# Attention scores by eight array tiles and the state's read by four column groups, from the third batch on

## The chip, the cores and the metric

The kernel runs on one core of one Trainium2 chip. The metric is the device time of one execution in microseconds (us); three runs of the kernel before gave a median of 699.95 us (699.75 to 700.57). A core has five engines that run beside each other and wait for each other by semaphores: TensorE (PE in the profile; its weight loads are PEld), VectorE (DVE), ScalarE (ACT), GpSimd (POOL) and SyncE (SP), which issues the DMA transfers.

## The reference

There are 8 batches of 8 heads, with 512 tokens of 64 numbers each, and a state of 32 rows per head. Attention goes both ways, and its result goes through two products with `h - tanh(h)` between them.

```python
scores = scale * np.matmul(x, state.transpose(0, 1, 3, 2))      # 512 x 32 per head
a = softmax(scores)                                             # over the state's rows
xread = np.matmul(a, state)
scores2 = scale * np.matmul(state, x.transpose(0, 1, 3, 2))     # 32 x 512 per head
a2 = softmax(scores2)                                           # over the tokens
sread = np.matmul(a2, x)                                        # 32 x 64 per head
x = concatenate([xread, sread], axis=2)                         # 4608 rows of 512 after a reshape
h = x @ w_in                                                    # 512 -> 2048
g = h - np.tanh(h)
out = g @ w_out                                                 # 2048 -> 512
```

## The kernel before, in words

The main loop goes over nine chunks of output rows: one for each batch's 512 tokens, and one for the 256 rows of all state reads. A chunk has 16 steps `f`, one for each 128 columns of the hidden layer. In each step `hidden` makes a tile `hps` of h (lines 355 to 357, six matmuls of 512 columns in three passes over float32r parts), ScalarE and VectorE make `g` of it (`finish`, lines 363, 89, 90), and `output` adds its share to the four tiles `ops` (lines 393 to 395, twelve matmuls of 512 columns). Between these stand the products of `m_units` (`mps`, lines 185 and 186), which make state @ w_in for later batches, and the attention of the next batch.

Attention of batch b works on half the heads at a time (`hf` is 0 or 1; tile names carry both digits, so `sps70` is batch 7, half 0). It has three kinds of TensorE work, all in plain float32, where one product is two records of the trace, one for each of its two passes:

- the scores `sps` (line 249): per half two products, each with the 64 columns of two heads as weights and 512 tokens as moving data. The weights `bdr` hold two heads' states in blocks, so that 128 rows carry two heads of 64 numbers, with zeros beside each block. The two products of a half stand in the two halves of the array's columns.
- the transposes `pps` (line 301), four per half,
- the state's read `rps` (line 309): per half four steps over 128 tokens, and in each two products of 64 weight columns and 128 moving columns, one in each half of the array's columns. Of the 64 x 128 block that results, two diagonal 32 x 64 blocks are used (line 315).

The scores go to PSUM tiles of the pool `ps_a`, which has two banks; ScalarE copies them out (line 255), and both softmaxes start from the copies. The tables of steps in the kernel say in which step each piece of attention is made. Within that, a scheduler that is part of the framework sets the order of the instructions on each engine when the program is built, by its own model of their times.

Of the kernel before, what the change touches and what calls it, by code (L numbers as in the profile page):

```python
# [9 lines left out]
F32 = mybir.dt.float32  # L10
# [9 lines left out]
P = 128  # L20
# [6 lines left out]
EPS = 1e-9  # L27
LAG = 2


@with_exitstack
def attention_ffn(ctx: ExitStack, tc: tile.TileContext, xT, xn, bd, sp, sm, sl, win, wout, xout, sout):
    """Two-way softmax attention between x and a small state, then h - tanh(h) between two products.

    Float32 operands of the products are split exactly into two float32r parts (hi + lo, 12 bits
    each); hi*hi + hi*lo + lo*hi carry float32's accuracy in three passes.

    x's read of the state is a @ state, so its product with w_in is taken as a @ (state @ w_in),
    whose contraction is half as long.

    win and wout are float32, or float64 as int64 words, which are rounded to float32 here.
    """
    nc = tc.nc
# [24 lines left out]
    sr = [cpool.tile([P, DM], F32, name=f"sr{g}") for g in range(2)]  # L68
    # state @ w_in, [half of the heads, head, row, column]; of the last two batches, two addends
    mdram = [  # L70
# [16 lines left out]
    def split(hi, lo, src, sub=None):  # L87
        """src = hi + lo."""
        nc.scalar.copy(hi, src)  # L89
        return (sub or nc.vector).tensor_sub(lo, src, hi)  # L90

    class Weight:
        """A [P, 512] part of a weight: load() issues its load, convert() makes float32 of it."""

# [15 lines left out]
        def steps(self, dst):  # L110
            """convert() by engines: Vector's first and second part, Scalar's, GpSimd's."""
            if self.src.dtype == F32:
                return [lambda: None] * 3 + [lambda: nc.gpsimd.tensor_copy(dst, self.raw)]
            low, high = self.raw[:, :, 0], self.raw[:, :, 1]
            u, i = dst.bitcast(U32), dst.bitcast(I32)
            r = pool.tile([P, 512], I32, tag="cr", name=f"{self.name}r", bufs=CB)
            return [
                # sign, the exponent's top bit; its other seven bits, 20 bits of the fraction
                lambda: nc.vector.tensor_scalar(u, high, 3, 0x3FFFFFFF, ALU.logical_shift_left, ALU.bitwise_and),  # L119
                lambda: nc.vector.scalar_tensor_tensor(u, high, 0xC0000000, u, ALU.bitwise_and, ALU.bitwise_or),  # L120
                # the fraction's last three bits, rounded; the sum may carry into the exponent
                lambda: nc.scalar.activation(r, low, AF.Copy, scale=2.0**-29),
                lambda: nc.gpsimd.tensor_add(i, i, r),
            ]

        def convert(self, dst):
            for step in self.steps(dst):
                step()

# [1 line left out]
    m_first = {}  # L131
# [9 lines left out]
    def m_first_two(q, p):  # L141
        """Heads 2p and 2p + 1 of the first two batches, in float32 as it stands."""
        k, c = p // 2, p % 2
        if p == 0:
            # The first batch's part stays on chip.
            m_first[q] = pool.tile([P, 2, 512], F32, tag="mr", name=f"mr0{q}", bufs=RRB)
        ps = bank(ps_a, f"mps0{q}{p}")
        nc.tensor.matmul(ps, sps[:, p], wfs[q, k][:, c], start=True, stop=True)
        nc.scalar.copy(m_first[q][64 * c : 64 * c + 64, k], ps[0:64])
        stage = pool.tile([P, 2, 512], F32, tag="stage", name=f"st0{q}{p}", bufs=SB)  # L150
        nc.scalar.copy(stage[64:128, 0], ps[64:128])
        nc.sync.dma_start(
            mdram[1][q][0][k, 2 * c : 2 * c + 2].rearrange("h n f -> (h n) f"), stage[64:128, 0]
        )

    def m_units(g):
        """Of the next four batches (g = 0) and of the last two (g = 1), by pairs of heads.

        The columns of the last two batches' product: half of them by the state's hi, half by its lo.
        """  # L160
        raw = pool.tile([P, H, P], F32, tag="stage", name=f"smr{g}", bufs=SB)
# [7 lines left out]
        for q in range(NQ):  # L169
            for k in range(2):  # L170
                w = pool.tile([P, 2, 512], F32, tag="wf", name=f"w1{g}{q}{k}", bufs=WB)
                nc.sync.dma_start(w, wf[q][:, 2 * k : 2 * k + 2])
                for c in range(2):
                    p = 2 * k + c
                    # Even heads: hi over lo; odd heads: lo over hi.
                    t = twins(f"wst{g}{q}{p}", [P, 2, 512], F32R)
                    split(t[0:64, 0], t[64:128, 0], w[0:64, c], WSUB)
                    split(t[64:128, 1], t[0:64, 1], w[64:128, c], WSUB)
                    hs = slice(2 * c, 2 * c + 2)
                    stage = pool.tile([P, 2, 512], F32, tag="stage", name=f"st{g}{q}{p}", bufs=SB)  # L180
                    for e in range(2):
                        h = 2 * p + e
                        ps = bank(ps_a, f"mps{g}{q}{h}")
                        if g == 0:
                            nc.tensor.matmul(ps, s[:, 1, h], t[:, e], start=True, stop=False)  # L185
                        nc.tensor.matmul(ps, s[:, 0, h], t[:, e], start=(g == 1), stop=True)  # L186
                        nc.scalar.copy(stage[:, e], ps)  # L187
                    for j in range(4):
                        dst = mdram[2 + j][q][0] if g == 0 else mdram[6 + j % 2][q][j // 2]
                        nc.sync.dma_start(dst[k, hs].rearrange("h n f -> n h f"), stage[32 * j : 32 * j + 32])  # L190
                    yield
# [38 lines left out]

# [1 line left out]
    def attention(b, aT):  # L232
        """Products in float32 as it stands, two at a time in halves of the array's columns."""
        bdr = pool.tile([P, 4, 64], F32, tag="bdr", name=f"bdr{b}", bufs=1)
        with tc.issue_after(loadlog[min(len(loadlog) - 1, XH1)]):
            nc.sync.dma_start(bdr, bd[b])
        xrs, ss, es = [], [], []
# [8 lines left out]
        def scores(hf):  # L246
            pss[hf] = bank(ps_a, f"sps{b}{hf}")
            for c in range(2):
                nc.tensor.matmul(pss[hf][64 * c : 64 * c + 64], bdr[:, 2 * hf + c], xrs[hf][:, c], start=True, stop=True)  # L249

        for hf in range(2):
            scores(hf)
            ps = pss[hf]
            s = pool.tile([P, 512], F32, tag="s", name=f"s{b}{hf}")
            nc.scalar.copy(s, ps)
            ss.append(s)
            # over the state's rows, for x's read: 32x32 blocks transposed
            e = pool.tile([P, 16, 32], F32, tag="e", name=f"e{b}{hf}")
# [21 lines left out]
    def state_read(b, ss):  # L280
# [3 lines left out]
        for hf in range(2):  # L284
            # over the tokens, for the state's read
            s = ss[hf]
# [17 lines left out]
            yield  # L304
            ps = bank(ps_a, f"rps{b}{hf}")[:, :P]
            for k in range(4):
                for c in range(2):
                    cs = slice(64 * c, 64 * c + 64)
                    nc.tensor.matmul(  # L309
                        ps[cs], pt[:, k, cs], xr[:, k, P * c : P * c + P], start=(k == 0), stop=(k == 3)  # L310
                    )
            for j in range(4):
# [3 lines left out]
                    sr[b // 4][32 * (b % 4) : 32 * (b % 4) + 32, 64 * h : 64 * h + 64],  # L316
                    ps[js, 64 * (j % 2) : 64 * (j % 2) + 64],
                    ri[js],
# [12 lines left out]

# [1 line left out]
    class Chunk:  # L333
# [9 lines left out]
        def hidden(self, f):  # L343
            """h, then g = h - tanh(h), of 128 columns of w_in; tokens along the free axis."""
            i, n = self.i, self.n
# [22 lines left out]
        def output(self, f):  # L368
# [3 lines left out]
            if self.i == B and f >= NFF - 2:  # L372
                # The end: the first tile is stored while the second is computed.
                if f == NFF - 1:
# [50 lines left out]

    # start: what the first chunk needs
    w0 = [
        [Weight(win[r * P : r * P + P, 512 * q : 512 * q + 512], f"w{q}{r}") for r in range(DM // P)]
        for q in range(NQ)
    ]  # L430
    # The first quarter by blocks of 128 columns.
    w0[0] = [
# [11 lines left out]

    # Loads in the order of their use: w_in's quarters ahead of w_out's rows.
    loads = iter(
# [7 lines left out]

    # The start, in this order on each engine.
    firstDVE = [None]
# [33 lines left out]
    def step(op):  # L490
# [70 lines left out]
        elif k == "R":  # L561
            # the second batch's part
            if j % 2 == 0:
# [141 lines left out]
```

## Time and profile before

| what | value |
|---|---|
| time, median of 3 runs | 699.95 us (699.75 to 700.57) |
| the profiled execution, first to last instruction | 699.7 us |
| PE busy | 670.6 us, 96% of the span |
| PEld busy | 530.2 us, 76% |
| DVE busy | 464.8 us, 66% |
| ACT busy | 378.4 us, 54% |
| POOL busy | 79.2 us, 11% |
| data moved by DMA | 99.68 MB, 142 GB/s on average |
| mean granted TensorE clock | 0.982 |

The busy times are of one profiled execution, whose own time is its span; the median of the runs is 0.25 us more. Engines overlap, so busy times don't add up to the span. A matmul's end is modelled in the trace and lies behind the start of the next one, so the pace of TensorE is read from starts, not from durations.

### The profile page before, as it was taken

How to read it: one execution, taken by the hardware profiler on the slowest of the kernel's cores; microseconds unless marked ns; L12 is line 12 of the kernel's file. 1: busy time of each engine (PE TensorE's matmuls, PEld its weight loads, DVE VectorE, ACT ScalarE, POOL GpSimd, SP SyncE). 2: the span in 40 equal slices, each digit the busy share in tenths (PEclk: the TensorE clock that was granted, in tenths of full speed). 3: DMA queues.
4: the chain of work that ended last, by engine and by line, in shares of the span. 5: the costliest groups of instructions: out<-in, count | busy, mean ns of one | idle time of the engine just before them, and what ended most of it. 6: DMA issues, size and time to landing. Idle time of an engine off the chain costs nothing.

```text
span 699.7 us, 8842 instructions
## 1 busy us (share of the span) xinstructions
PE 670.6 (96%) x3146; PEld 530.2 (76%) x3146; DVE 464.8 (66%) x755; ACT 378.4 (54%) x663; POOL 79.2 (11%) x59
## 2 busy tenths in 40 slices
PE   5888995999999999999999999999999999999997
PEld 2555663888778887888788878887888788888896
DVE  5998899965695559556776558545864596444442
ACT  3876866566674655447656545543543354333442
POOL 3766656200000000000000000000000000000000
PEclk9989899899999999999999999999999999999999
DMA  8887762553554554245635632563241312001400
GB/s 298 291 298 273 250 248 100 186 199 111 152 168 141 164 163 128 90 151 151 186 120 163 170 99 65 177 189 111 77 173 61 112 69 91 30 1 38 143 31 31
DMA packets 46316, 99.68 MB, mean 142 GB/s; under 512 B 6208, under 2 KB 12096, under 8 KB 46272
## 3 DMA queue, kind: packets, MB, share of 16 engines
q1 hardware_dynamic: 46272, 99.11, 43.9%
q8 instruction: 25, 0.41, 0.3%
q14 instruction: 19, 0.16, 0.1%
HBM read 67.11 MB, written 31.98 MB: 142 GB/s over the span
## 4 chain that ended last, share of the span: by engine, by line
PE 84%; DVE 9%; ACT 2%; issue 2%; POOL 1%; DMA 1%; SPq 0%; ACTq 0%; DVEq 0%; POOLq 0%
PE ops L395 17%; PE ops L393 17%; PE ops L394 16%; PE hps L356 9%; PE hps L355 9%; PE hps L357 8%; PE rps L309 2%; PE mps L186 2%; DVE w L120 2%; PE sps L249 2%; PE mps L185 1%; DMA w01d<-in_win 1%; PE pps L301 1%; DVE wor L119 1%; DVE w L119 1%
## 5 line engine op out<-in xcount | busy, mean ns | idle before, releaser
L393 PE MATMUL ops<-wo,g 128*128 128x512 f32 x544 | 211.1, 398 | 4.8 <-ACT wo L89 2.9
L394 PE MATMUL ops<-wo,g 128*128 128x512 f32 x544 | 215.1, 395 | 0.2 <-POOL wo L90 0.2
L395 PE MATMUL ops<-wo,g 128*128 128x512 f32 x544 | 208.9, 394 | 0.0
L363 ACT ACTIVATE t<-hps 128x512 f32<-128x512 f32 (+1 forms) x142 | 81.3, 573 | 151.3 <-PE hps L357 150.7
L363 DVE TENSOR_TENSOR t<-hps,t 128x512 f32<-128x512 f32 (+1 forms) x142 | 93.2, 658 | 102.3 <-ACT t L363 101.3
L393 PEld LDWEIGHTS ops<-wo,g 128*128 128x128 f32 x544 | 103.0, 190 | 32.7 <-ACT wo L89 4.6
L90 DVE TENSOR_TENSOR g<-t,g 128x512 fp32r<-128x512 f32 (+1 forms) x142 | 100.2, 706 | 39.9 <-ACT g L89 37.9
L89 ACT CAST g<-t 128x512 fp32r<-128x512 f32 (+1 forms) x142 | 84.7, 596 | 72.7 <-DVE t L363 69.8
L394 PEld LDWEIGHTS ops<-wo,g 128*128 128x128 f32 x544 | 103.0, 189 | 23.3 <-issue 2.3
L395 PEld LDWEIGHTS ops<-wo,g 128*128 128x128 f32 x544 | 103.4, 190 | 22.5 <-issue 0.5
L355 PE MATMUL hps<-aT,m 128*128 128x512 f32 x248 | 99.5, 402 | 3.3 <-DVE t L363 1.7
L357 PE MATMUL hps<-aT,m 128*128 128x512 f32 x248 | 98.4, 399 | 0.7 <-DVE m L90 0.7
L356 PE MATMUL hps<-aT,m 128*128 128x512 f32 x248 | 98.5, 398 | 0.0
L355 PEld LDWEIGHTS hps<-aT,m 128*128 128x128 f32 x248 | 47.3, 191 | 15.3 <-ACT m L89 2.4
L90 DVE TENSOR_TENSOR wst<-w,wst 64x512 fp32r<-64x512 f32 x64 | 46.0, 718 | 19.2 <-ACT wst L89 15.9
L356 PEld LDWEIGHTS hps<-aT,m 128*128 128x128 f32 x248 | 47.5, 191 | 11.7 <-issue 2.2
L357 PEld LDWEIGHTS hps<-aT,m 128*128 128x128 f32 x248 | 47.4, 191 | 11.7 <-DVE m L90 1.5
L90 DVE TENSOR_TENSOR m<-mr,m 128x1024 fp32r<-128x1024 f32 x31 | 39.9, 1287 | 9.4 <-ACT m L89 9.3
L187 ACT COPY st<-mps 128x512 f32<-128x512 f32 x64 | 36.7, 587 | 14.6 <-PE mps L186 14.3
L89 ACT CAST wst<-w 64x512 fp32r<-64x512 f32 x64 | 39.6, 619 | 2.3 <-issue 1.5
L89 ACT CAST m<-mr 128x1024 fp32r<-128x1024 f32 x31 | 32.3, 1042 | 3.6 <-DMA mr<-md 3.4
L90 POOL TENSOR_TENSOR wo<-wor,wo 128x512 fp32r<-128x512 f32 x16 | 25.3, 1586 | 6.0 <-ACT wo L89 6.0
(216 smaller groups left out, 661.7 us busy)
## 6 DMA issues: line engine op xcount, KB each, us to landing
md<-st SPq DMA_DIRECT2D x144, 128.0 KB, 2.3
mr<-md SPq DMA_DIRECT2D x28, 512.0 KB, 4.0
xT<-in_xT SPq DMA_DIRECT2D x16, 512.0 KB, 4.4
xn<-in_xn SPq DMA_DIRECT2D x16, 512.0 KB, 4.8
w<-wf SPq DMA_DIRECT2D x16, 512.0 KB, 4.9
out_x<-ob SPq DMA_DIRECT2D x32, 256.0 KB, 2.2
wn<-wf SPq DMA_DIRECT2D x8, 512.0 KB, 3.9
ml<-md SPq DMA_DIRECT2D x8, 512.0 KB, 3.6
```

The source lines that it names most:

```text
L89: nc.scalar.copy(hi, src)
L90: return (sub or nc.vector).tensor_sub(lo, src, hi)
L119: lambda: nc.vector.tensor_scalar(u, high, 3, 0x3FFFFFFF, ALU.logical_shift_left, ALU.bitwise_and),
L120: lambda: nc.vector.scalar_tensor_tensor(u, high, 0xC0000000, u, ALU.bitwise_and, ALU.bitwise_or),
L187: nc.scalar.copy(stage[:, e], ps)
L355: nc.tensor.matmul(ps, mhi[k][:, cols], ahi[:, k], start=(k == 0), stop=False)
L356: nc.tensor.matmul(ps, mhi[k][:, cols], alo[:, k], start=False, stop=False)
L357: nc.tensor.matmul(ps, mlo[k][:, cols], ahi[:, k], start=False, stop=(k == nk - 1))
L363: tanhs.append((nc.scalar.activation(t, ps, AF.Tanh).ins, nc.vector.tensor_sub(t, ps, t).ins))
L393: nc.tensor.matmul(o, g[:, 0, tok], wo[:, f, 0], start=(f == 0), stop=False)
L394: nc.tensor.matmul(o, g[:, 0, tok], wo[:, f, 1], start=False, stop=False)
L395: return nc.tensor.matmul(o, g[:, 1, tok], wo[:, f, 0], start=False, stop=(f == NFF - 1)).ins
```

## The change

Batches 0 and 1 stay as they are (`LONE = 2`). From batch 2 on:

- Scores: each product takes one head alone, with its 64 numbers as rows and its 32 state rows as weight columns. The first four heads stand in the upper 64 rows of the array and the last four in the lower 64, each in a column group of its own, so that eight products stand in eight tiles of 64 rows and 32 columns. All eight are issued by one function, and both `sps` banks are taken at once. The weights have no zeros any more, and their load is half as large (64 KB instead of 128 KB). The inputs are laid out for that on the host.
- State's read: each step of 128 tokens has four products of 32 weight columns and 64 moving columns, one in each column group, instead of two of 64 and 128. The useful blocks are the same, and no others are computed.

```diff
-        bdr = pool.tile([P, 4, 64], F32, tag="bdr", name=f"bdr{b}", bufs=1)
+        if b < LONE:
+            bdr = pool.tile([P, 4, 64], F32, tag="bdr", name=f"bdr{b}", bufs=1)
+        else:
+            bdr = pool.tile([P, 4, NS], F32, tag="bdr", name=f"bdr{b}", bufs=1)
         with tc.issue_after(loadlog[min(len(loadlog) - 1, XH1)]):
-            nc.sync.dma_start(bdr, bd[b])
+            nc.sync.dma_start(bdr, bd[b] if b < LONE else bh[b - LONE])
...
+        def all_scores():
+
+            pss.update({hf: bank(ps_a, f"sps{b}{hf}") for hf in range(2)})
+            for j in range(4):
+                for hf in range(2):
+                    rs = slice(64 * hf, 64 * hf + 64)
+                    nc.tensor.matmul(
+                        pss[hf][32 * j : 32 * j + 32], bdr[rs, j], xrs[j // 2][rs, j % 2], start=True, stop=True
+                    )
+
+        if b >= LONE:
+            all_scores()
         for hf in range(2):
-            scores(hf)
+            if b < LONE:
+                scores(hf)
             ps = pss[hf]
...
-            ps = bank(ps_a, f"rps{b}{hf}")[:, :P]
+
+            w = 2 if b < LONE else 1
+            ps = bank(ps_a, f"rps{b}{hf}")[:, : 64 * w]
             for k in range(4):
-                for c in range(2):
-                    cs = slice(64 * c, 64 * c + 64)
+                for c in range(4 // w):
+                    cs = slice(32 * w * c, 32 * w * c + 32 * w)
                     nc.tensor.matmul(
-                        ps[cs], pt[:, k, cs], xr[:, k, P * c : P * c + P], start=(k == 0), stop=(k == 3)
+                        ps[cs], pt[:, k, cs], xr[:, k, 64 * w * c : 64 * w * c + 64 * w], start=(k == 0), stop=(k == 3)
                     )
```

The scheduler moves instructions as a result. On TensorE, in the last steps of chunk 1, the two halves of batch 2's scores stood in two places before, with 25 other rows between them:

```order
L355 MATMUL hps1_12_1722<-aT1_586,m13_1719 128x512
L249 MATMUL sps20_1586<-xT20_1519,bdr2_1517 64x512 x2
L356 MATMUL hps1_12_1722<-aT1_586,m13_1719 128x512
...
L355 MATMUL hps1_13_1747<-aT1_586,m13_1719 128x512
L249 MATMUL sps21_1640<-xT21_1521,bdr2_1517 64x512 x2
L356 MATMUL hps1_13_1747<-aT1_586,m13_1719 128x512
```

Now all eight products stand together, in the place of the first half:

```order
L375 MATMUL hps1_12_1726<-aT1_586,m13_1723 128x512
L262 MATMUL sps20_1586<-xT20_1519,bdr2_1517 32x512 x2
L262 MATMUL sps20_1586<-xT21_1521,bdr2_1517 32x512
L262 MATMUL sps21_1587<-xT20_1519,bdr2_1517 32x512 x2
L262 MATMUL sps21_1587<-xT21_1521,bdr2_1517 32x512
L262 MATMUL sps20_1586<-xT21_1521,bdr2_1517 32x512
L262 MATMUL sps21_1587<-xT21_1521,bdr2_1517 32x512
L376 MATMUL hps1_12_1726<-aT1_586,m13_1723 128x512
```

Two places became one. Batch 7's scores, on TensorE in chunk 6, stood in one place before, behind step 11's `hps`:

```order
L357 MATMUL hps6_11_4766<-aT6_4113,m62_4688 128x512
L249 MATMUL sps70_4779<-xT70_4667,bdr7_4665 64x512 x2
L249 MATMUL sps71_4790<-xT71_4669,bdr7_4665 64x512 x2
L393 MATMUL ops6_0_4527<-wo_77,g6_9_4726 128x512
```

Now two of the eight products stand far ahead, each alone among the matmuls of step 1, and six remain at the old place:

```order
L414 MATMUL ops6_0_4627<-wo_77,g6_1_4587 128x512
L262 MATMUL sps70_4879<-xT70_4767,bdr7_4765 32x512
L415 MATMUL ops6_0_4627<-wo_77,g6_1_4587 128x512
L262 MATMUL sps71_4880<-xT70_4767,bdr7_4765 32x512
L413 MATMUL ops6_1_4628<-wo_77,g6_0_4562 128x512
...
L377 MATMUL hps6_11_4866<-aT6_4193,m62_4788 128x512
L262 MATMUL sps70_4879<-xT70_4767,bdr7_4765 32x512
L262 MATMUL sps71_4880<-xT70_4767,bdr7_4765 32x512
L262 MATMUL sps70_4879<-xT71_4769,bdr7_4765 32x512
L262 MATMUL sps71_4880<-xT71_4769,bdr7_4765 32x512
L262 MATMUL sps70_4879<-xT71_4769,bdr7_4765 32x512
L262 MATMUL sps71_4880<-xT71_4769,bdr7_4765 32x512
L413 MATMUL ops6_0_4627<-wo_77,g6_9_4826 128x512
```

One place became three. The scores of batches 3, 5 and 6 stand in one place each before and after; those of batch 4 in two places, with four products each after. The twelve reads (two per batch) stand as one block each, before with 8 and after with 16 products.

## Rows read from the trace of the kernel before

**Rows 1.** The page: busy time by engine, PE by slice, the chain's shares.
```profile
PE 670.6 (96%) x3146; PEld 530.2 (76%) x3146; DVE 464.8 (66%) x755; ACT 378.4 (54%) x663; POOL 79.2 (11%) x59
...
PE   5888995999999999999999999999999999999997
...
PE 84%; DVE 9%; ACT 2%; issue 2%; POOL 1%; DMA 1%; SPq 0%; ACTq 0%; DVEq 0%; POOLq 0%
```

**Rows 2.** Busy time by stretch: PE, PEld, DVE, ACT, POOL (instructions), clock, DMA share, GB/s.
```profile
180.00:640.00 460.00, 460.00 (x2173) 369.15 (x2173) 294.60 (x502) 238.90 (x411) 0.00 (x0) 1.00 0.39 121
...
188.00:208.00 20.00, 20.00 (x89) 14.78 (x88) 18.45 (x36) 14.46 (x27) 0.00 (x0) 1.00 0.57 177
```

**Rows 3.** Groups by line, PE, 180 to 640 us: records, busy us, mean ns.
```profile
L309 PE MATMUL rps<-xn,p2t 128*64 128x128 f32 x192 | 13.1, 279 | 0.0
L249 PE MATMUL sps<-xT,bdr 128*64 128x512 f32 x48 | 12.1, 609 | 0.0
L301 PE MATMUL pps<-ident,s 128*128 128x128 f32 x48 | 7.9, 279 | 0.0
```

**Rows 4.** Timeline, PE, two regular matmuls nine steps apart: start us, us, line.
```profile
139.03 0.39 PE L393 MATMUL ops<-wo,g 128*128 128x512 f32 x1
...
141.07 0.39 PE L393 MATMUL ops<-wo,g 128*128 128x512 f32 x1
```

**Rows 5.** Timeline, PE, around the scores of one half (batch 2).
```profile
188.90 0.39 PE L355 MATMUL hps<-aT,m 128*128 128x512 f32 x1
189.22 1.08 PE L249 MATMUL sps<-xT,bdr 128*64 128x512 f32 x4
190.23 0.50 PE L356 MATMUL hps<-aT,m 128*128 128x512 f32 x1
190.56 0.39 PE L185 MATMUL mps<-wst,sms 128*128 128x512 f32 x1
```

**Rows 6.** Timeline, PE, around the scores of both halves (batch 7).
```profile
554.31 0.39 PE L357 MATMUL hps<-aT,m 128*128 128x512 f32 x1
554.62 1.94 PE L249 MATMUL sps<-xT,bdr 128*64 128x512 f32 x8
556.49 0.51 PE L393 MATMUL ops<-wo,g 128*128 128x512 f32 x1
556.83 0.40 PE L394 MATMUL ops<-wo,g 128*128 128x512 f32 x1
```

**Rows 7.** Timeline, PE, around one read (batch 4, second half).
```profile
369.71 0.39 PE L395 MATMUL ops<-wo,g 128*128 128x512 f32 x1
370.03 1.09 PE L309 MATMUL rps<-xn,p2t 128*64 128x128 f32 x16
371.05 0.50 PE L186 MATMUL mps<-wst,sms 128*128 128x512 f32 x1
371.39 0.40 PE L355 MATMUL hps<-aT,m 128*128 128x512 f32 x1
```

**Rows 8.** Timeline, PE: a read's first 0.02 us; a double read; one product of the whole array.
```profile
363.62 0.33 PE L309 MATMUL rps<-xn,p2t 128*64 128x128 f32 x2
...
135.19 1.97 PE L309 MATMUL rps<-xn,p2t 128*64 128x128 f32 x32
137.09 0.50 PE L356 MATMUL hps<-aT,m 128*128 128x512 f32 x1
137.43 0.40 PE L357 MATMUL hps<-aT,m 128*128 128x512 f32 x1
...
14.77 0.83 PE L537 MATMUL mps<-w,sps 128*128 128x128 f32 x6
```

**Rows 9.** One line's records in short windows: the sequencer's waits, and a weight load.
```profile
L309 PEldq EVENT_SEMAPHORE  x1: 51/51/51, 135.2 to 135.2; - x1
...
L185 PEldq EVENT_SEMAPHORE  x1: 51/51/51, 137.5 to 137.5; - x1
...
L185 PEld LDWEIGHTS mps<-wst,sms x1: 188/188/188, 141.1 to 141.1; 128*128 128x128 f32 x1
```

More of the change, by code (lines that the diff above doesn't have):

```diff
@@ L28, with attention_ffn @@
 LAG = 2
+LONE = 2
 @with_exitstack
-def attention_ffn(ctx: ExitStack, tc: tile.TileContext, xT, xn, bd, sp, sm, sl, win, wout, xout, sout):
+def attention_ffn(ctx: ExitStack, tc: tile.TileContext, xT, xn, bd, bh, sp, sm, sl, win, wout, xout, sout):
     nc = tc.nc
@@ L316, in state_read @@
                     sr[b // 4][32 * (b % 4) : 32 * (b % 4) + 32, 64 * h : 64 * h + 64],
-                    ps[js, 64 * (j % 2) : 64 * (j % 2) + 64],
+                    ps[js, 64 * (j % w) : 64 * (j % w) + 64],
                     ri[js],
@@ L669 @@
     xT = c(x.reshape(B, 2, 2, 2, S, D).transpose(0, 1, 3, 5, 2, 4).reshape(B, 2, P, 2, S))
+    xT[LONE:] = x[LONE:].reshape(B - LONE, 2, 2, 2, S, D).transpose(0, 2, 1, 5, 3, 4).reshape(B - LONE, 2, P, 2, S)
     xn = c(x.reshape(B, 2, 4, 4, P, D).transpose(0, 1, 4, 3, 2, 5).reshape(B, 2, P, 4, 256))
@@ L676 @@
         bd[:, e, :, :, e] = sT[:, e::2].transpose(0, 2, 1, 3)
-    bd = bd.reshape(B, P, 4, 64)
+    bd = bd.reshape(B, P, 4, 64)[:LONE]
+    bh = c(sT[LONE:].reshape(B - LONE, 2, 4, D, NS).transpose(0, 1, 3, 2, 4).reshape(B - LONE, P, 4, NS))
     sp = np.zeros((2, D, 4, 2, 2, NS), x.dtype)
@@ L691 @@
     nc = bacc.Bacc("TRN2", target_bir_lowering=False, num_devices=1)
-    arrays = {"in_xT": xT, "in_xn": xn, "in_bd": bd, "in_sp": sp, "in_sm": sm, "in_sl": sl, "in_win": win, "in_wout": wout}
+    arrays = {"in_xT": xT, "in_xn": xn, "in_bd": bd, "in_bh": bh, "in_sp": sp, "in_sm": sm, "in_sl": sl, "in_win": win, "in_wout": wout}
     args = [
```

## The prediction

> **What bounds the kernel now.** I read the page first. TensorE is busy for 96% of the span, its digits stand at 9 from the seventh slice to the last but one, and it holds 84% of the chain that ended last [rows 1]. The view by stretches says where: from 180 to 640 us PE is busy for all 460 us at the full granted clock, with VectorE at 294.6 and ScalarE at 238.9 us [rows 2]. So in this stretch every microsecond that TensorE is spared comes off the time, as long as nothing else gets in its way. All that the change touches lies in it, since batch 2's scores start at 189.2 us [rows 5]. The groups of PE say how much there is: 48 records of scores, 192 of reads [rows 3], that is 24 and 96 products of two passes each.
>
> What such a block costs is read from starts. Regular matmuls of 512 columns follow each other every (141.07 - 139.03) / 9 = 0.227 us [rows 4]. A block's price is the time from the start of the last regular matmul ahead of it to the start of the second one behind it, less two of those steps (0.45):
> - scores of one half, 190.56 - 188.90 - 0.45 = 1.21 us [rows 5];
> - scores of both halves in one place, 556.83 - 554.31 - 0.45 = 2.07 us [rows 6];
> - one read, 371.39 - 369.71 - 0.45 = 1.23 us [rows 7].
>
> The double block has two more rounds than the single one (a round is one pass in each of the two tiles that run side by side), so a round of scores takes (2.07 - 1.21) / 2 = 0.43 us, and 1.21 - 2 x 0.43 = 0.35 us are **fixed**: the array runs empty ahead of the block and behind it, and the first weights load uncovered. For the read, 32 records take 1.97 us where 16 take 1.09 [rows 7, 8], so a round of two takes 0.88 / 8 = 0.11 us and the fixed part is 1.23 - 8 x 0.11 = 0.35 us again.
>
> **What a second tile costs now.** Nothing: a read's first two records both start at 363.62 and end together after 0.33 us, and products of the whole array with the same 128 moving columns follow at (0.83 - 0.28) / 5 = 0.11 us, no faster than the pairs [rows 8]; 0.28 is the mean of a record of that size [rows 3]. In the built program both passes of a product stand one behind the other, so the second tile's first pass goes past the waiting second pass of the first tile. The Trainium skill says otherwise: "TensorE: Matmul & The Clock Gate", section "The mechanism" of the part on packing, has matmuls start and end strictly in program order. By that rule two products of two passes would take three rounds. The trace has two [rows 5], so it does not agree.
>
> **Scores, part by part.** Before: batches 2 and 4 stand in two blocks each, 3, 5, 6 and 7 in one (the two kinds are those of [rows 5, 6]; the built order shows which batch has which): 4 x 1.21 + 4 x 2.07 = 13.1 us. After, if all eight tiles run side by side, a block of eight has two rounds instead of four; a round keeps its 0.43 us, since 512 columns still pass. I take 0.35 + 0.86 + 0.02 = 1.23 us, the 0.02 for six later starts of at most 0.01 us each [rows 8], less a shorter weight load. Batches 2, 3, 5, 6: 4 x 1.23 = 4.9. Batch 4 keeps two blocks: 2 x 1.21 = 2.4. Batch 7 is torn into three: each lone product still has its two rounds and the fixed part, 2 x 1.2, and the other six cost 1.23, together 3.6 against 2.07 before, a loss of 1.6. Sum 11.0; **gain 2.1 us**.
>
> **Reads.** Twelve blocks. After, 16 products in four tiles are 32 records in eight rounds, each of 64 moving columns instead of 128, so 0.055 instead of 0.11 us if columns alone count. 0.35 + 8 x 0.055 = 0.79 instead of 1.23; **gain 12 x 0.44 = 5.2 us**. No row shows so short a round. Bounds: no gain from below, and a loss if instructions can't be supplied fast enough (first rival).
>
> **At nothing.** The copies, the softmaxes and the scaling of `sr` keep their number and size; the weights' load is halved and DMA is busy for 0.39 of that stretch [rows 2]. The new order brings both halves of batch 2 together on VectorE, which is its fullest place: 18.45 of 20 us [rows 2]. The same work now has about 20 - 1.2 us, so a few tenths are left; if TensorE waits there after all, I price that at up to 1 us. What would be late next is `g`, and TensorE with it. All eight scores now wait for both banks of `ps_a`; in batch 7 the lone two hold both from step 1 to step 11 of chunk 6, and in the built order no other product asks for that pool in between.
>
> **Sum.** 699.7 - 2.1 - 5.2 = 692.4 us for the profiled execution. Its span lies 0.25 us under the median of the runs, so the forecast for the median is **692.6 us**; own range 691.5 to 694.
>
> **The rivals.**
> *A, the supply of instructions.* A read has 32 products' worth of weight loads and matmuls in 0.44 us. The sequencer works ahead: it passed a wait of line 185 at 137.5, and the load behind that wait started at 141.1 [rows 9], 3.6 us or 16 matmuls later. So about half a block stands ready and 16 pairs must be supplied while it runs. How fast can that go? Between the waits at 135.2 and 137.5 it supplied what ran from the middle of the double read to 141.1, 16 pairs of the read and about 18 regular ones: 34 in 2.3 us, at least one per 0.068 us [rows 8, 9]. At that bound a block costs 0.35 + 16 x 0.068 = 1.44, a loss of 0.21 each, 2.5 in all: 700.3 us. At the pace that the reads have now, one per 0.055 us, they gain nothing: 697.8. Below 0.027 the forecast stands. Nothing shows that the sequencer was at its limit at 0.068, since its stock was nearly full at both times. The Trainium skill has a figure for it: "TensorE: Matmul & The Clock Gate", section "Back-to-back issue gap", gives matmuls of up to 64 columns a floor of about 25 ns each. As an estimate from that page, 32 of them would take 0.8 us instead of 0.44, and the time would be 697. No run here shows it.
> *B, four at once, not eight.* The upper and the lower 64 rows of one column group may not overlap; no row shows row tiles. Blocks of eight then have four rounds, 2.07: batch 2 gains 0.35, batches 3, 5, 6 and 4 nothing, batch 7 loses 2 x 1.2 + 2.07 - 2.07 = 2.4; the reads keep their 5.2: 699.95 - 3.2 = 696.8 us.
> *C, slower: two at once.* All that the rows show is two tiles at a time. If that is the most, a block of eight has eight rounds, 0.35 + 3.44 = 3.8: batch 2 loses 1.4, batches 3, 5 and 6 lose 1.7 each, batch 4 2 x 0.86, batch 7 2.4 + 2.9 - 2.1 = 3.2; the reads stay as they are: 711.4 us. Even at three at once it would be slower: the reads gain 12 x 0.29 = 3.5, but blocks of eight take 2.64 and the scores lose about 5. Against it: the second tile is free, with no sign of a shared path.
> *D, strict program order*, a pass waiting for all passes ahead of it: eight products take nine rounds, 4.2 us, 16 take 17. The scores lose 1.8 + 3 x 2.15 + 2.6 + 3.7 = 14.5 and the reads 0.7: 715 us. Against it: the two rounds of [rows 5] where it would have three. For it: the engine must now look past up to 14 waiting records and not two. It is the rule of the Trainium skill's page named above.
>
> **How the numbers follow.** Forecast, waits in the new order among it, 64%; A 16%; B 11%; C 6%; D 3%. A change under 0.2% (1.4 us) can hardly be told from none here. Faster by more: the forecast, B and most of A, 87%. Within it: the slow end of A, 4%. Slower: C and D, 9%. The range 691.2 to 697.9 holds the forecast, B and two thirds of A, some 85%.
>
> **What would show it.** Right: blocks of `sps` with 16 records in about 1.3 us between their first start and the next regular one behind them, pairs of starts giving way to groups of eight within 0.06 us; `rps` blocks of 32 records whose rounds start 0.055 us apart; PE without idle time from 180 us on; two lone `sps` products in chunk 6 at 1.2 us each. Wrong: rounds of reads stretching behind the first 16 products (A), scores' second half starting 0.86 us late (B), four or more rounds (C, D), or PE waiting for VectorE between 188 and 210 us.

## The result: 692.3 us against 700.3 us, and the profile after

Measured beside each other, the kernel before takes 700.26 us (median of 4 runs, 699.75 to 700.84) and the changed one 692.30 us (4 runs, 692.02 to 693.16): a ratio of 0.9885, 95% interval 0.9871 to 0.9899, so 7.1 to 9.0 us less. The forecast was 692.6, its own range 691.5 to 694. In a second set of runs the changed kernel had the ratio 0.9895 (0.9879 to 0.9910).

The page after, its lines that answer to [rows 1]:

```profile
PE 658.9 (95%) x3386; PEld 520.4 (75%) x3386; DVE 462.5 (67%) x755; ACT 378.4 (55%) x663; POOL 78.3 (11%) x59
...
PE   5888996999999999999999999999999999999997
...
PE 82%; DVE 9%; ACT 4%; DMA 2%; issue 2%; POOL 1%; SPq 0%; ACTq 0%; POOLq 0%; DVEq 0%
```

TensorE is still what bounds the kernel, with more instructions and less time. The view by stretches, to set beside [rows 2] (the second stretch is the one in which batch 2's scores now stand together):

```profile
180.00:640.00 460.00, 460.00 (x2453) 370.03 (x2452) 297.11 (x508) 241.10 (x415) 0.00 (x0) 1.00 0.39 122
187.00:207.00 20.00, 20.00 (x102) 15.65 (x101) 18.32 (x38) 14.75 (x28) 0.00 (x0) 1.00 0.53 169
```

PE has no idle time from 180 to 640 us, at the full clock, and so none in the stretch where both halves of batch 2 now meet on VectorE. The groups by line in the stretch of [rows 3]:

```profile
L262 PE MATMUL sps<-xT,bdr 64*32 64x512 f32 x96 | 9.6, 601 | 0.0
L329 PE MATMUL rps<-xn,p2t 128*32 128x64 f32 x384 | 7.8, 222 | 0.0
L319 PE MATMUL pps<-ident,s 128*128 128x128 f32 x48 | 7.8, 279 | 0.0
```

Twice as many records of scores and of reads take 9.6 instead of 12.1 us and 7.8 instead of 13.1 us; the transposes beside them stay at 7.8. These busy times leave out a part of what a block costs (1.09 us busy for eight scores, which cost 1.22), so the blocks' prices come from starts again. Around the eight scores of batch 2, and how many of their records had started at 188.16 and at 188.19 us:

```profile
187.40 0.39 PE L375 MATMUL hps<-aT,m 128*128 128x512 f32 x1
187.72 1.09 PE L262 MATMUL sps<-xT,bdr 64*32 64x512 f32 x16
188.74 0.50 PE L376 MATMUL hps<-aT,m 128*128 128x512 f32 x1
189.08 0.39 PE L377 MATMUL hps<-aT,m 128*128 128x512 f32 x1
...
187.72 0.66 PE L262 MATMUL sps<-xT,bdr 64*32 64x512 f32 x8
...
187.72 1.06 PE L262 MATMUL sps<-xT,bdr 64*32 64x512 f32 x11
```

The price, as in the prediction, is 189.08 - 187.40 - 0.45 = 1.23 us (1.22 in whole nanoseconds), with two rounds: eight records start in the first 0.05 us, none follows until after 188.16, and the other eight come from there on. Four products cost 1.21 before [rows 5], and eight cost 2.07 [rows 6].

Around a read (batch 4, the half that [rows 7] show), and the records that had started at 364.255, at 364.42 and at 364.588 us:

```profile
363.85 0.39 PE L415 MATMUL ops<-wo,g 128*128 128x512 f32 x1
364.17 0.65 PE L329 MATMUL rps<-xn,p2t 128*32 128x64 f32 x32
364.75 0.50 PE L187 MATMUL mps<-wst,sms 128*128 128x512 f32 x1
365.09 0.40 PE L375 MATMUL hps<-aT,m 128*128 128x512 f32 x1
...
364.17 0.30 PE L329 MATMUL rps<-xn,p2t 128*32 128x64 f32 x5
...
364.17 0.47 PE L329 MATMUL rps<-xn,p2t 128*32 128x64 f32 x17
...
364.17 0.63 PE L329 MATMUL rps<-xn,p2t 128*32 128x64 f32 x29
```

365.09 - 363.85 - 0.45 = 0.79 us instead of 1.23. The 5th, 17th and 29th record are the first of the second, fifth and eighth round. Each row's time runs from the block's start to that record's end, so the rounds are (0.63 - 0.30) / 6 = 0.055 us apart. Two decimals are too coarse for the halves of the block. The starts in whole nanoseconds say that the second round comes 80 ns behind the first and each later one 56 ns behind the one before it, in both halves alike.

Batch 7's scores, torn into three:

```profile
510.28 0.39 PE L414 MATMUL ops<-wo,g 128*128 128x512 f32 x1
510.60 1.04 PE L262 MATMUL sps<-xT,bdr 64*32 64x512 f32 x2
511.57 0.50 PE L415 MATMUL ops<-wo,g 128*128 128x512 f32 x1
512.00 1.04 PE L262 MATMUL sps<-xT,bdr 64*32 64x512 f32 x2
512.98 0.50 PE L413 MATMUL ops<-wo,g 128*128 128x512 f32 x1
513.31 0.40 PE L414 MATMUL ops<-wo,g 128*128 128x512 f32 x1
...
546.87 0.39 PE L377 MATMUL hps<-aT,m 128*128 128x512 f32 x1
547.19 1.08 PE L262 MATMUL sps<-xT,bdr 64*32 64x512 f32 x12
548.19 0.50 PE L413 MATMUL ops<-wo,g 128*128 128x512 f32 x1
548.53 0.39 PE L414 MATMUL ops<-wo,g 128*128 128x512 f32 x1
```

From the matmul ahead of the two lone products to the second one behind them, 513.31 - 510.28 = 3.03 us, three regular steps of 0.227 us are contained, so both together cost 2.35 us, 1.17 each. The six others cost 548.53 - 546.87 - 0.45 = 1.21. That is 3.56 us for batch 7 instead of the 2.07 of [rows 6].

**A clean measure.** Ahead of batch 2's scores TensorE runs the same 679 matmuls in the same order in both traces, and of the DMA transfers only the load of batch 2's weights differs. Yet that start lies at 189.22 us before [rows 5] and at 187.72 after: runs of one and the same kernel differ there, as the repeat below shows. From that start to the end of the span the traces agree far better: 699.7 - 189.2 = 510.5 us before, 690.5 - 187.7 = 502.8 after. So the change is worth 7.7 us by the traces. Summed over their blocks, scores went from 13.1 to 10.8 us and reads from 13.7 to 8.4: 2.3 and 5.3, together 7.6 of the 7.7. (Six of the reads have transposes right behind them, whose shorter steps make their prices 0.17 us lower, before and after alike: 1.06 and 0.61 us instead of 1.23 and 0.79.)

### The profile page after: what moved, and what is told of

The parts are those of the page before. It is cut to its first block, busy times and chain, and to the rows that moved or that the text cites. A ratio compares the mean times of both kernels' runs of the same rounds, so it can differ in the third digit from the quotient of the medians.

```text
span 690.5 us, 9315 instructions
## 1 busy us (share of the span) xinstructions
PE 658.9 (95%) x3386; PEld 520.4 (75%) x3386; DVE 462.5 (67%) x755; ACT 378.4 (55%) x663; POOL 78.3 (11%) x59
## 4 chain that ended last, share of the span: by engine, by line
PE 82%; DVE 9%; ACT 4%; DMA 2%; issue 2%; POOL 1%; SPq 0%; ACTq 0%; POOLq 0%; DVEq 0%
PE ops L415 16%; PE ops L413 16%; PE ops L414 16%; PE hps L376 9%; PE hps L377 9%; PE hps L375 9%; PE mps L187 2%; DVE w L121 2%; PE sps L262 1%; PE rps L329 1%; PE mps L186 1%; PE pps L319 1%; DVE g L91 1%; DVE wor L120 1%; DMA wo4d<-in_wout 1%
## 5 line engine op out<-in xcount | busy, mean ns | idle before, releaser
L91 DVE TENSOR_TENSOR m<-mr,m 128x1024 fp32r<-128x1024 f32 x31 | 40.9, 1321 | 10.8 <-ACT m L90 10.0
```

## The experiments

The same measure for every kernel, from its trace (us):

| kernel | batch 2's scores start | span | from there to the end |
|---|---|---|---|
| before | 189.2 | 699.7 | 510.5 |
| changed | 187.7 | 690.5 | 502.8 |
| changed, again | 189.2 | 691.9 | 502.8 |
| scores alone | 189.7 | 696.5 | 506.8 |
| reads alone | 189.7 | 694.9 | 505.2 |
| batch 7 in one block | 188.8 | 689.3 | 500.5 |
| the same, again | 189.8 | 690.3 | 500.5 |
| four groups, 128 columns each | 186.9 | 693.6 | 506.7 |
| reads tile by tile | 189.7 | 701.4 | 511.7 |
| from batch 1 on | 192.2 | 695.0 | 502.8 |
| two steps a turn | 187.6 | 691.1 | 503.5 |
| three steps a turn | 188.8 | 696.5 | 507.7 |

**The two parts apart.** The changed kernel with the old reads, and the kernel before with the new reads:

```diff
-            w = 2 if b < LONE else 1
+            w = 2
```

> The new scores with the reads of before. In the built order batch 7's scores stand as one lone product and a block of seven. Theory (TensorE is the bound from 180 us on, and a block costs 0.35 us plus its rounds): batch 2 gains 1.2, batches 3, 5 and 6 gain 0.85 each, batch 4 nothing, batch 7 loses 0.35, so 3.4 us less than before, near 696.8; the blocks of eight have two rounds of 0.43 us. If upper and lower rows took turns (B): blocks of eight with four rounds, and no gain or a loss. If the gains of the two parts don't add up, another engine has become the bound.

```diff
-            ps = bank(ps_a, f"rps{b}{hf}")[:, :P]
+            w = 2 if b < 2 else 1
+            ps = bank(ps_a, f"rps{b}{hf}")[:, : 64 * w]
...
-                for c in range(2):
-                    cs = slice(64 * c, 64 * c + 64)
+                for c in range(4 // w):
+                    cs = slice(32 * w * c, 32 * w * c + 32 * w)
...
-                        ps[cs], pt[:, k, cs], xr[:, k, P * c : P * c + P], start=(k == 0), stop=(k == 3)
+                        ps[cs], pt[:, k, cs], xr[:, k, 64 * w * c : 64 * w * c + 64 * w], start=(k == 0), stop=(k == 3)
...
```

> The new reads with the scores of before. Theory: twelve blocks at 0.79 instead of 1.23 us, 5.3 us less than before, near 694.9. If instructions were supplied too slowly (A): rounds that stretch behind the 16th product, and 698 to 702. With the scores alone it should add up to the whole change, apart from batch 7, whose scores are cut into three places in the whole change and two in the scores alone.

Measured: scores alone 696.75 us, ratio 0.9953 (0.9941 to 0.9966); reads alone 695.11 us, 0.9928 (0.9915 to 0.9940). That is 3.3 and 5.0 us, together 8.3 against 8.0 for the whole, each with an interval of some 0.9 us to either side. By the traces reads alone are worth 510.5 - 505.2 = 5.3 us and scores alone 3.7. The scores' share is larger here than in the changed kernel because batch 7 was torn less: one lone product (1.17 us) and a block of seven (1.21), 1.2 us less than the three places of the changed kernel. The rest of its blocks cost what they cost there. So the parts add up: 5.3 + 3.7 = 9.0 us, and the whole with that 1.2 us is 8.9.

**Batch 7 in one block.** The changed kernel, with batch 7's scores held back until the last `output` matmul issued so far:

```diff
-        if b >= LONE:
+        if b == 7:
+            with tc.issue_after(lastadd[0]):
+                all_scores()
+        elif b >= LONE:
             all_scores()
...
-            return nc.tensor.matmul(o, g[:, 1, tok], wo[:, f, 0], start=False, stop=(f == NFF - 1)).ins
+            lastadd[0] = nc.tensor.matmul(o, g[:, 1, tok], wo[:, f, 0], start=False, stop=(f == NFF - 1)).ins
+            return lastadd[0]
...
```

> The whole change, but batch 7's scores are issued behind the output matmuls of step 8, so that all eight stand in one place. Theory: two lone products at 1.27 and 1.29 us and a block of six at 1.21 become one block of 1.22, so 2.5 us less than the changed kernel, near 689.8. If a lone product's price were hidden by other waits, no change: 692.3.

Measured: 691.04 us, 0.9866 (0.9850 to 0.9881). It and the changed kernel were then timed once more, side by side:

> The changed kernel as it stands, beside the three runs of this set, so that they can be compared on one chip: 692.3 us, ratio 0.9885 to before.

> Batch 7's scores in one place, once more, beside the changed kernel. Theory: 2.5 us less than the changed kernel (two lone products and a block of six, 3.76 us, become one block of 1.22). If part of that were hidden, about 1.3 us, as a comparison over two sets of runs has it.

Changed 693.11 us (691.88 to 694.06), 0.9895 (0.9879 to 0.9910); batch 7 in one block 691.53 (690.72 to 692.06), 0.9872 (0.9859 to 0.9886). The block, in the second trace:

```profile
546.60 0.39 PE L380 MATMUL hps<-aT,m 128*128 128x512 f32 x1
546.91 1.09 PE L262 MATMUL sps<-xT,bdr 64*32 64x512 f32 x16
547.93 0.50 PE L416 MATMUL ops<-wo,g 128*128 128x512 f32 x1
548.27 0.39 PE L417 MATMUL ops<-wo,g 128*128 128x512 f32 x1
```

548.27 - 546.60 - 0.45 = 1.22 us for all eight, instead of 3.56 for the three places: 2.34 us less. From batch 2's scores to the end both traces have 500.5 us, 2.3 less than the changed kernel's 502.8. So the price of tearing is shown where it was put; the 2.5 us that were expected had counted the stretch between the two lone products (511.57 to 512.00) in the price of both, which is 0.2 us too much. In the timed runs 1.3 and 1.6 us are seen, but the intervals of the ratios are each about 2 us wide, and the place ahead of batch 2's scores moves by more than 1 us between runs: 187.7 and 189.2 in two traces of the changed kernel. It is the fastest kernel of this study by both measures.

**What a round costs.** The changed kernel with four column groups in the reads, each again with 128 moving columns:

```diff
-            ps = bank(ps_a, f"rps{b}{hf}")[:, : 64 * w]
+            ps = bank(ps_a, f"rps{b}{hf}")[:, :P]
...
-                        ps[cs], pt[:, k, cs], xr[:, k, 64 * w * c : 64 * w * c + 64 * w], start=(k == 0), stop=(k == 3)
+                        ps[cs], pt[:, k, cs], xr[:, k, P * (w * c // 2) : P * (w * c // 2) + P], start=(k == 0), stop=(k == 3)
...
-                    ps[js, 64 * (j % w) : 64 * (j % w) + 64],
+                    ps[js, 64 * (j % 2) : 64 * (j % 2) + 64],
```

> The whole change, but the reads' four column groups each pass 128 moving columns instead of 64 (half of what they compute is unused). Batch 7's scores stand in two places (one and seven). Theory (columns alone set a round): eight rounds of 0.11 us in four tiles, 1.23 us a block as before, so the reads' whole gain of 5.3 us goes, less 1.3 for batch 7's scores: 696.3, as with the scores alone. If the number of products counts beside the columns, a block is dearer than 1.23 and the time is above 696.8.

Measured: 696.55 us, 0.9942 (0.9930 to 0.9955). A read in its trace:

```profile
365.16 0.39 PE L415 MATMUL ops<-wo,g 128*128 128x512 f32 x1
365.48 1.08 PE L329 MATMUL rps<-xn,p2t 128*32 128x128 f32 x32
366.49 0.50 PE L187 MATMUL mps<-wst,sms 128*128 128x512 f32 x1
366.82 0.40 PE L375 MATMUL hps<-aT,m 128*128 128x512 f32 x1
```

366.82 - 365.16 - 0.45 = 1.21 us, the old price (1.23, [rows 7]) with as many records as the changed kernel has. So four tiles instead of two, with twice the weight loads and matmuls, cost nothing here; the moving columns of a round, 128 or 64, make the whole difference of 0.42 us.

**From batch 1 on.** One more batch in the new form:

```diff
-LONE = 2
+LONE = 1
```

> The change from the second batch on instead of the third. Batch 1's attention lies between 80 and 135 us, where TensorE waits for other engines for about a tenth of the time. Theory: what TensorE is spared there comes back as waits, and in the built order batch 1's scores stand in three places instead of two; so within 1 us of the changed kernel.

Measured: 697.05 us, 0.9957 (0.9942 to 0.9971), some 4 us slower than the changed kernel: a miss. From batch 2's scores to the end it takes 502.8 us like the changed kernel, so all of the loss lies ahead of them: they start at 192.2 where the other traces have 186.9 to 189.8. The changed kernel by stretches from 60 to 140 us, columns as in [rows 2], and then this one:

```profile
60.00:80.00 20.00, 16.78 (x61) 11.14 (x59) 18.63 (x22) 13.49 (x24) 12.20 (x8) 0.91 0.64 223
80.00:100.00 20.00, 19.17 (x78) 13.15 (x76) 17.57 (x23) 15.13 (x27) 13.75 (x10) 1.00 0.79 282
100.00:120.00 20.00, 13.90 (x68) 9.89 (x68) 19.24 (x28) 14.05 (x24) 10.99 (x7) 1.00 0.38 135
120.00:140.00 20.00, 18.12 (x95) 14.56 (x96) 19.43 (x36) 11.44 (x20) 5.08 (x4) 0.91 0.57 179
```

```profile
60.00:80.00 20.00, 17.70 (x69) 11.89 (x69) 17.93 (x21) 14.60 (x26) 14.11 (x11) 1.00 0.74 261
80.00:100.00 20.00, 16.64 (x73) 11.20 (x72) 15.01 (x15) 10.28 (x18) 14.55 (x11) 1.00 0.65 226
100.00:120.00 20.00, 12.56 (x74) 8.68 (x72) 19.59 (x34) 14.74 (x27) 11.97 (x9) 0.83 0.47 159
120.00:140.00 20.00, 17.61 (x108) 13.52 (x109) 17.85 (x33) 11.73 (x21) 0.43 (x1) 0.91 0.59 185
```

Here TensorE is not the bound in either kernel; from 80 to 135 us it is idle for 16% of the time in the changed one, more than the tenth that was expected. Added up over the four stretches, it is busy for 67.97 us in the changed kernel and for 64.51 in this one: 3.5 us less. Batch 1's scores now stand in three places, at 76.3, 82.1 and 96.7 us, where they stood in two, at 79.2 and 93.2. The view of waits has TensorE's longest one of this stretch at the line of the transposes (us in total, times, longest):

```profile
PE pps L319 <- ACT s L310: 5.9, 1, 5.9
```

The changed kernel has no wait at that line there; its longest one of this stretch has 3.6 us. The wait ends at 111.6 us. The granted clock falls from 2.4 to 1.2 GHz in the course of it and stays there until 116.4, which is the 0.83 against 1.00 in the third stretch; in the first it is the other way round, 1.00 against 0.91. Over the four stretches the clock is at the lower level for some 10 us instead of 7. As an estimate from these rows, 3.2 us more at half the clock delay TensorE's work by 1.6 us at most. Which part of the 4 us is the torn scores, the wait and the clock was not taken apart.

**How far TensorE looks past a waiting pass.** The changed kernel with the reads' products in another order, one column group after the other, nothing else changed:

```diff
-            for k in range(4):
-                for c in range(4 // w):
+            for c, k in [(c, k) for c in range(4) for k in range(4)] if w == 1 else [(c, k) for k in range(4) for c in range(2)]:
+                if True:
```

> The changed kernel with the reads' 16 products issued column group by column group: a group's four steps, that is eight passes in a row, before the next group begins. The work is the same. It tells how far TensorE looks past passes that must wait. If it looks past any number: 0.79 us a block and 692.3 us. If it sees about 33 instructions (weight loads and matmuls), in which two groups' passes stand, and these make room in order: two groups at a time, 16 rounds, 1.23 us a block, and 697.6. If it looks past next to none (D): 29 rounds of 0.055 us, 1.95 us a block, and 706.

Measured: 702.01 us (11 runs), ratio 1.0019 (1.0010 to 1.0028), 8.9 us more than the changed kernel in the same set. That lies between the second and the third expectation, a miss for all three. A read in its trace:

```profile
369.57 0.39 PE L415 MATMUL ops<-wo,g 128*128 128x512 f32 x1
369.88 1.40 PE L329 MATMUL rps<-xn,p2t 128*32 128x64 f32 x32
371.21 0.50 PE L187 MATMUL mps<-wst,sms 128*128 128x512 f32 x1
371.55 0.39 PE L375 MATMUL hps<-aT,m 128*128 128x512 f32 x1
```

371.55 - 369.57 - 0.45 = 1.53 us instead of 0.79, and 12 x 0.74 = 8.9: neither free nor one pass at a time throughout. The records that had started 0.25 us behind a block's first, in the tile-by-tile kernel:

```profile
363.18 0.47 PE L329 MATMUL rps<-xn,p2t 128*32 128x64 f32 x5
```

Five, where the changed kernel has 17 (above). The second of them starts 0.08 us behind the first, and the others 0.056 us apart. The trace doesn't name the column groups, but the starts in nanoseconds fall into four lines of eight with this same rhythm, which are taken for the groups. So the five are the first group's alone, and the second group's first record comes 6 ns after the first group's fifth, when three of its eight are left waiting, the third group's again behind the second's fifth, and so on. Two theories fit that, and two more orders tell them apart, with two and three steps of a group in a row (each diff against the changed kernel's two loops):

```diff
+            for c, k in [(c, k) for h in range(2) for c in range(4) for k in (2 * h, 2 * h + 1)] if w == 1 else [(c, k) for k in range(4) for c in range(2)]:
```

> The changed kernel, with the reads' products issued two steps of a column group in a row (four passes), then the next group's two, and so on, and then the other two steps of each. In the tile-by-tile kernel the second group's first pass came when three passes of the first were left waiting. Theory 1, each tile has a line of its own, with room for three waiting passes, and only a full line holds up what is behind it: four passes are one running and three waiting, so nothing is held up, all four groups run side by side, a block takes 0.8 to 0.9 us, and the time is within 1.5 us of the changed kernel's, 692.5 to 694. Theory 2, three waiting passes in all can be passed, whatever their tile: two groups fill that, so two run at a time, a block takes some 1.2 us, and the time is 697.5 to 698.5.

```diff
+            for c, k in [(c, k) for h in ((0, 1, 2), (3,)) for c in range(4) for k in h] if w == 1 else [(c, k) for k in range(4) for c in range(2)]:
```

> The changed kernel, with the reads' products issued three steps of a column group in a row (six passes), then the next group's three, and at the end the fourth step of each. Theory 1, a line for each tile with room for three waiting passes: each group holds up the next until its own third pass has started, some 0.14 us, so the fourth group starts some 0.42 us late, a block takes 1.15 to 1.2 us, and the time is 696.5 to 697.8. Theory 2, three waiting passes in all: 699 to 702, near the tile-by-tile kernel.

Measured: two steps 693.05 us, 0.9900 (0.9885 to 0.9915); three steps 697.66 us, 0.9968 (0.9959 to 0.9977), both as theory 1 has it and outside what theory 2 has. The records that had started some 0.25 us behind a block's first, with two and with three steps a turn:

```profile
364.39 0.45 PE L329 MATMUL rps<-xn,p2t 128*32 128x64 f32 x16
...
367.28 0.47 PE L329 MATMUL rps<-xn,p2t 128*32 128x64 f32 x7
```

Sixteen are four of each group; seven are five of the first group and two of the second. The read with three steps a turn:

```profile
366.96 0.39 PE L415 MATMUL ops<-wo,g 128*128 128x512 f32 x1
367.28 1.06 PE L329 MATMUL rps<-xn,p2t 128*32 128x64 f32 x32
368.27 0.50 PE L187 MATMUL mps<-wst,sms 128*128 128x512 f32 x1
368.61 0.39 PE L375 MATMUL hps<-aT,m 128*128 128x512 f32 x1
```

368.61 - 366.96 - 0.45 = 1.20 us (1.15 to 1.2 expected). The starts in nanoseconds: the second group begins at 142, 6 after the first group's third record, again with three of six left; the third group at 283 and the fourth at 425. With two steps a turn, where a group has one pass running and three waiting, the four begin 13 ns apart, at 0, 13, 27 and 40, and the block costs 0.83 us. So in these reads each tile can have three passes waiting and others still go past them, and a fourth holds up everything behind it. That is shown for four column groups of all 128 rows; no run has more than one waiting pass of a tile in the scores' eight tiles.

## Why the prediction was right

- **The bound.** PE has no idle time from 180 to 640 us in either kernel, the view of waits shows none of PE's in that stretch, and 7.6 of the 7.7 us by the traces are the blocks' own. Scores alone and reads alone add up. The gain was forecast as 7.3 us. That the forecast of the time is only 0.3 us off has luck in it, since the start of batch 2's scores alone moves by more between runs of one kernel.
- **Scores.** The block of eight was put at 1.23 us and costs 1.22; four products were put at 1.21 and cost 1.19; lone ones 1.2 and 1.17, as in the kernel with scores alone. So 10.8 us instead of the 11.0 predicted, and a gain of 2.3 instead of 2.1. That a lone product costs nearly as much as eight is what the fixed part and two rounds said. One sign was misstated: from a block's first start to the next regular one behind it the prediction named about 1.3 us, but that is 1.02 for the eight (187.72 to 188.74), as it was 1.01 for four in [rows 5].
- **Reads.** The round of 0.055 us was what no row had shown. It is 0.056, and the wide reads show that it goes by moving columns and not by instructions. 0.79 was predicted for a block and 0.79 measured. The gain of 5.2 came out as 5.3.
- **The fixed part.** Its size holds in every block here, but its two causes were argued. For the uncovered first load the trace has this: a regular load starts some 0.22 us ahead of its matmul, and the first one of batch 2's block (187.72) and the one behind it (188.74) start within 2 ns of theirs. How the 0.35 us divide between that and an array that runs empty stays open.
- **At nothing.** VectorE's 18.45 of 20 us [rows 2] became 18.32 and PE did not wait; the up to 1 us set aside for it was not needed. That this is VectorE's fullest place was misread: 340 to 360 us has 19.01 before, and 335 to 355 has 19.14 after. PE doesn't wait there either.
- **A, the supply of instructions.** Its mark was rounds that stretch behind the first 16 products' records. The rounds of the second half are no longer than those of the first. By the estimate from the Trainium skill ("TensorE: Matmul & The Clock Gate", section "Back-to-back issue gap", about 25 ns for each small matmul) 32 of them would have taken 0.8 us; the trace has 32 records in eight rounds of 0.055 us, one per 14 ns, so across tiles that floor does not hold here.
- **B and C.** Eight records of scores start in the first 0.05 us and only two rounds follow each other, so neither four nor two at once.
- **D, strict program order.** Nine rounds would have shown in the same rows, and there are two. But its doubt was sound: the engine does not look past any number of waiting passes. In the changed order a tile's pass has at most one waiting pass of each other tile of its step ahead of it; tile by tile, the same products lose all that the change gained. That the two passes of a product stand one behind the other in the program is read from no row, so the changed kernel alone doesn't show that a pass goes past another. The tile-by-tile kernel does: there a group starts while three passes issued ahead of it wait. The Trainium skill's rule (same page, section "The mechanism": matmuls start and end in program order) does not agree with that.
- **One sentence was wrong.** That the profiled execution's own time is its span, 0.25 us under the median. Each run of the changed kernel lies about 1.8 us above its span (692.26 against 690.5), so by the same 1.8 us the profiled execution of before took about 701.5 us, 1.5 above the median. Its late start of batch 2's scores fits that. Since the sum is a difference, this moved nothing.

## What to carry to other kernels

Where TensorE is the bound, price a block of small products by starts (last regular matmul ahead to second one behind), split it into a fixed part (0.35 us here) and rounds, and count rounds by moving columns: idle columns and zero weights are then worth taking out, and a product that is torn from its block pays fixed part and rounds anew. Issue the products of side-by-side tiles in turn and not tile by tile: the same 16 products cost 0.79 us or 1.53. And what pays in a stretch that TensorE binds can lose time in one where it waits: batch 1 in the new form lost 4 us, though what lost it was not taken apart.

## What the runs showed of the hardware that was not expected

- Eight tiles' first passes start within 0.05 us, 6 to 7 ns apart; the reads' four start 6 to 7 ns apart too, and 13 where four passes of a tile stand in a row. With more passes of one tile in a row, in the reads, three may wait without holding up other tiles: groups began when exactly three were left, with eight passes in a row (behind the fifth) and with six (behind the third), and with four nothing was held up.
- From batch 2's scores to the end, traces of the same kernel agree within some 0.01 us (502.77, 502.76 and, with batch 1 changed too, 502.77), while their start moves by 1.5 us. Compared over that stretch, a trace tells apart what the whole time cannot.
